# First products of a transform on 64x64 quarters of the array, and maxima spread through free PSUM columns

## The chip, the cores and the metric

One core of a Trainium2 chip runs the kernel alone. The metric is device time in microseconds (us) of one execution; three timed runs of the kernel before gave 3619.89, 3620.4 and 3622.17 us, median 3620.4. The rows below come from one further, profiled execution. PE is TensorE (PEld its weight loads), DVE VectorE, ACT ScalarE, POOL GpSimd, SP the SyncE that issues DMAs.

## The reference

`x` is 8 batches of 3072 x 256. All in float32 accuracy, which the kernel reaches with pairs of fp16 numbers (hi, lo) and three products for each product.

```
X = rfft(x, axis=1)                                  # along the 3072
Yr = Xr @ w_r - Xi @ w_i + b_r ;  Yi = Xr @ w_i + Xi @ w_r + b_i
Y  = soft_threshold(Yr, 0.01) + 1j * soft_threshold(Yi, 0.01)
x  = irfft(Y)                                        # "attn" out, 24576 tokens x 256
x  = (sigmoid(x @ w_gate) * (x @ w_val)) @ w_out     # width 1536
# then 8 experts: tokens with x @ w_skip > 0 go to argmax(x @ w_gate2)
out = x + gate * relu(x @ w1[e]) @ w2[e]             # routed tokens only
```

## The kernel before

The program has three stages. **Boot** transforms batch 0 and prepares the weights. The **main stage** runs 768 *units*: a unit is one of 12 blocks of 128 hidden columns for one of 64 chunks of 384 tokens (8 chunks a batch). `gv` of a unit makes the gate and the value (12 products of 384 columns, tiles `pg`), `out` of the unit two before it makes the output (9 products of 265 columns, tile `pz`); the hidden values go through `h` and `hh` on DVE and ACT. The **last stage** runs the experts in blocks of 512 tokens (`ph`, `py`).

In the main stage a scheduler written in Python, at build time, puts steps of five background tasks behind the products of each unit, up to a budget: `attn` (the transform of the next batch), `y` (its last inverse step, chunk by chunk), `route`, `prep` (expert weights) and `start`. Each task is a generator; a `yield` ends a step, and `k.due` says from which unit on the next may run. Every engine works its instructions in the order in which they were written. When `y` comes to a new batch whose transform is not all written, it names `attn`, and the scheduler writes steps of `attn` at once until it is done.

`attn` of a batch goes through its 8 chunks of `x` (`bound`: the largest magnitude; `scale`; `halve`: hi and lo into `xh`; `cols`: products with the matrix `c1` into a bank of `pa`, then hi and lo into `ah`, and by DMA to `asc` in DRAM). Then it takes 13 groups of frequencies, three stages in a software pipeline: `freq` (tile `al`, product with `f2s`, result `x`), `mix_pair` or `mix` (products with `wri` and `wse`, soft threshold on DVE through `yf`, `yc`, halves `yn`, four DMAs into `yh`), and `inv` of the group before (product of `yh`, halves `zh`, DMA to `zsc`). `y` loads `zt` from `zsc`.

A maximum over partitions is needed before each scaling. `allpow` rounds the per-partition maximum to a power of two on DVE (two instructions on tile `pp`) and its `spread`, written at the end of the task's next step, is one product `pm<-idb,pp` of 128 columns into a bank of `pa` and a DVE maximum over the 128 columns. `pa` has two banks, shared with all products of the tasks.

Before, `c1` for one of the 32 column groups is 96 x 96 and block diagonal: rows are two halves h of 48 time points, columns two halves of 48 results, so half of its entries serve no purpose.

Of the kernel before, what the change touches and what calls it, by code (L numbers as in the profile page):

```python
# [38 lines left out]
def make_consts():  # L39
# [9 lines left out]
    c1 = np.zeros((2, N1, HN, 2, 2, NK))  # L49
# [3 lines left out]
    for h in range(2):  # L53
        t = th[:, h * HN:(h + 1) * HN]
        c1[h, :, :, 0, h, :] = np.cos(t)
        c1[h, :, :, 1, h, :] = -np.sin(t)
        c2[0, h, :, :, h, :] = (w * np.cos(t)).transpose(2, 1, 0)
        c2[1, h, :, :, h, :] = (-w * np.sin(t)).transpose(2, 1, 0)
        c1[h, :, :, :, h, 0] = alt.T[:, None, :]
        c2[:, h, 0, :, h, :] = w / 2 * alt[:, None, :]  # L60
    c1 = np.stack(hl(c1.reshape(96, HN, 96)), 2)
# [24 lines left out]
    at = np.arange(128).reshape(2, 2, HN).transpose(2, 0, 1).reshape(128)  # L86
    f2 = [m.reshape(128, 128)[at] for m in (fx, su, sv)] + [m.reshape(128, 128)[:, at] for m in (fi, si)]
# [78 lines left out]
def allpow(k, out, in_, lo):  # L166

    p = k.pt.tile([128, 1], F32, tag="pp", name="pp", bufs=6)
    pow2(k, p, in_, lo)

    def spread():
        ps = k.pa.tile([128, 512], F32, tag="pa", name="pm")[:, :128]
        w = p.bitcast(BF16)[:, 1:2].broadcast_to([128, 128])
        k.nc.tensor.matmul(ps, w, k.idb, start=True, stop=True)
        k.V.tensor_reduce(out, ps, axis=AX.X, op=ALU.max)

    (k.late if k.boot else k.later).append(spread)
# [26 lines left out]
def split_far(k, hi, lo, src, scale):  # L204

    n = src.free_size()
    tmp = k.sp0.tile([128, n], F32, tag="tmp", name="tmp", bufs=2)
# [6 lines left out]
def task(gen):  # L214
    return [gen, [], []]


def step(k, r):
# [3 lines left out]
    last, k.later = r[2], []  # L222
# [3 lines left out]
    for f in last:  # L226
        f()
    r[1], r[2] = k.late, k.later
    if got == -1 or isinstance(got, str):
        for f in r[1] + r[2] if got == -1 else ():  # L230
            f()
        return got
# [9 lines left out]
def setup_consts(k):  # L242
    nc, cp, d = k.nc, k.cp, k.d
    ld = lambda name, shape, dt: cp.tile(shape, dt, name=name)
    k.c1 = ld("c1", [4 * NK, HN, 2, 96], F16)
# [225 lines left out]
def attn_gen(k, b):  # L471
# [6 lines left out]
    V.memset(mx[:, 0], 0.0)  # L478
    V.memset(px[:, 2], 0.0)
    x32, xh, ah, xs, als, yhs = k.x32, {}, {}, {}, {}, {}  # L480
# [14 lines left out]
    def load(i):  # L495

        e, c = b + i // NC, i % NC
        if e < NB:
            xv = k.d.x[e].rearrange("(n h j) d -> h n j d", h=2, j=HN)
            pool = k.sp0 if e == 0 and c % 4 == 3 else k.xp  # L500
            x32[e, c] = pool.tile([96, NJ, D], F32, tag="x32", name=f"x32_{e}_{c}", bufs=3 if pool is k.xp else 1)
            for h in range(2):
                nc.sync.dma_start(x32[e, c][h * N1:(h + 1) * N1], xv[h, :, c * NJ:(c + 1) * NJ, :])

    def bound(c, h=None):
        if h is None:
            absmax(k, mx[:96, 0, c:c + 1], x32[b, c], axis=AX.XY)
        else:
            absmax(k, (px if h else mx)[:96, h, c:c + 1], x32[b, c][:, 2 * h:2 * h + 2], axis=AX.XY)
        if h == 1:  # L510
            V.tensor_tensor(mx[:96, 0, c:c + 1], mx[:96, 0, c:c + 1], px[:96, 1, c:c + 1], op=ALU.max)
        if h != 0:
            allpow(k, px[:, 0, c:c + 1], mx[:, 0, c:c + 1], 2.0**-40)

    def scale(c):
        inv_pow2(k, px[:, 1, c:c + 1], px[:, 0, c:c + 1], 9)

    def halve(c):
        xh[c] = k.wp.tile([96, 2, NJ, D], F16, tag="xh", name=f"xh_{b}_{c}")
        x, s = x32.pop((b, c)), px[:96, 1, c:c + 1]  # L520
# [5 lines left out]
    def cols(c, t):  # L526
        if t == 0:
            ah[c] = k.wp.tile([4 * NK, NJ, 2, D], F16, tag="ah", name=f"ah_{b}_{c}")
        out = ah[c][:, 2 * t:2 * t + 2]
        ps = bank()[:4 * NK]  # L530
        for jj in range(2):
# [5 lines left out]
        pv = ps.rearrange("p (j e) -> p j e", j=2)  # L537

        def evict():
            (split_far if b == 0 and t else split)(k, out[:, :, 0], out[:, :, 1], pv, 2.0**-7)  # L540
            if t == 1:
                nc.sync.dma_start(asc[:, c * NJ:(c + 1) * NJ], ah[c])

        after(evict)

    def amax(c):
        absmax(k, px[:4 * NK, 2, c:c + 1], ah.pop(c)[:, :, 0], axis=AX.XY)

    f2s = k.wp.tile([128, 3, 2, 128], F16, tag="f2s", name=f"f2s_{b}", bufs=1)
# [10 lines left out]
    def first_cols():  # L560

        pps, pss = {}, {}

        def top(c):
            absmax(k, mx[:96, 0, c:c + 1], x32[b, c], axis=AX.XY)
# [9 lines left out]

        def products(c):
            ah[c] = k.wp.tile([4 * NK, NJ, 2, D], F16, tag="ah", name=f"ah_{b}_{c}")
            x = xh.pop(c)
            pss[c] = [pool.tile([128, 512], F32, tag=tag, name="ps")[:4 * NK] for pool, tag in ((k.pg, "pg"), (k.pa, "pa"))]
            for j in range(NJ):  # L580
                for i, (a, w) in enumerate(PROD):
                    nc.tensor.matmul(
                        pss[c][j // 2][:, j % 2 * D:(j % 2 + 1) * D], k.c1[:, c * NJ + j, a, :], x[:, w, j, :],
                        start=i == 0, stop=i == 2,
                    )

        def evict(c):
# [1043 lines left out]
```

## Time and profile before

| | |
|---|---|
| median of three timed runs | 3620.4 us |
| profiled execution | 3608.6 us, of which the span from first to last instruction is 3606.8 us |
| PE busy | 3396.6 us, 94% of the span |
| DVE / ACT / POOL busy | 66% / 45% / 17% |
| stages (span's clock) | boot to 215 us, main to 2921 us, experts to the end |

Busy PE is matmul time with overlapping tails, so 94% does not say that PE is 94% used; what counts is where PE's idle time stands and what ended it.

### The profile page before, as it was taken

The page shows a single profiled execution, that of the slowest core. Times are in us where ns is not written, and L with a number is a line of the kernel's source. Part 1 is how long each engine was busy: PE and PEld are TensorE (multiplying, and loading weights), DVE is VectorE, ACT ScalarE, POOL GpSimd, SP SyncE. Part 2 cuts the span into 40 slices and gives each one's busy share as a digit, 9 for nine tenths or more (in the row PEclk, how much of TensorE's full clock was granted, in tenths as well). Part 3 has the DMA queues.
Part 4 walks back from the last instruction along what each step waited for, and adds up shares of the span by engine and source line. Part 5 has one row for each costly group of instructions (what it writes and reads, how often), then busy time and mean ns, then how long its engine had stood idle before and what let it go on. Part 6 is the DMA issues. An engine that isn't in the chain of part 4 may idle for free. (4 is left out here: it accounts for less than half of the span.)

```text
span 3606.8 us, 67115 instructions
## 1 busy us (share of the span) xinstructions
PE 3396.6 (94%) x26190; PEld 2428.2 (67%) x26190; DVE 2369.0 (66%) x5577; ACT 1639.4 (45%) x3220; POOL 625.9 (17%) x613
## 2 busy tenths in 40 slices
PE   5589999998999999999999999999999999999997
PEld 4457766676766666666666767676666766667675
DVE  7767677767766766676767676767645455665553
ACT  4545544554454544454444444544434343333332
POOL 2500100120012001200120012001200121333332
PEclk9889999999999999999999999999999999999999
DMA  6333333223332332232323322323211021444442
GB/s 174 113 103 98 96 88 96 87 78 93 99 99 57 104 92 74 78 88 87 94 64 97 96 74 79 99 67 91 70 32 41 28 86 48 154 145 142 162 164 93
DMA packets 220977, 336.06 MB, mean 93 GB/s; under 512 B 37633, under 2 KB 181763, under 8 KB 213392
## 3 DMA queue, kind: packets, MB, share of 16 engines
q1 hardware_dynamic: 204480, 305.43, 28.0%
q0 software_dynamic: 15744, 25.99, 2.4%
q8 instruction: 206, 3.38, 0.4%
q14 instruction: 115, 0.94, 0.1%
q10 hardware_dynamic: 432, 0.33, 0.0%
HBM read 177.99 MB, written 134.09 MB: 87 GB/s over the span
## 5 line engine op out<-in xcount | busy, mean ns | idle before, releaser
L965 PE MATMUL pg<-yT,wgv 128*128 128x384 f16 x9216 | 1634.5, 327 | 5.3 <-ACT yT L149 3.0
L965 PEld LDWEIGHTS <-wgv 128*128 128x128 f16 x9216 | 892.2, 98 | 536.3 <-issue 16.0
L998 PE MATMUL pz<-wo,hh 128*128 128x265 f16 x6912 | 919.0, 277 | 19.0 <-DVE hh L149 16.2
L149 DVE TENSOR_TENSOR hh<-h,hh 128x384 f16<-128x384 f32 x768 | 438.5, 571 | 589.7 <-ACT hh L149 588.1
L998 PEld LDWEIGHTS <-hh 128*128 128x128 f16 x6912 | 675.5, 98 | 213.8 <-DVE hh L149 21.8
L149 ACT ACTIVATE sg<-pg,ys 128x384 f32<-128x384 f32 x768 | 443.7, 578 | 697.5 <-PE pg L965 695.7
L149 DVE SCALAR_TENSOR_TENSOR h<-pg,sg 128x384 f32<-128x384 f32 x768 | 421.8, 549 | 4.7 <-PE pg L965 4.7
L149 ACT CAST hh<-h 128x384 f16<-128x384 f32 x768 | 386.8, 504 | 44.2 <-DVE h L149 43.6
L149 POOL TENSOR_TENSOR x<-sm,x 128x256 f16<-128x256 f32 x77 | 55.0, 714 | 1826.9 <-ACT x L149 836.5
L1095 POOL DMA_INDIRECT lst<-rent,ridx x192 | 198.2, 1032 | 528.4 <-DVE rent L149 277.2
L1320 PE MATMUL ph<-zT,we 128*128 128x512 f16 (+3 forms) x1344 | 268.2, 358 | 4.8 <-DVE h L149 4.1
L1340 PE MATMUL py<-we,h 128*128 128x256 f16 x2400 | 271.1, 273 | 0.9 <-DVE h L149 0.9
L1340 PEld LDWEIGHTS <-h 128*128 128x128 f16 x2400 | 233.5, 98 | 32.6 <-DVE h L149 1.2
L1320 PEld LDWEIGHTS <-we 128*128 128x128 f16 x1344 | 128.1, 98 | 135.8 <-issue 10.7
L149 PEld LDWEIGHTS <-x 128*128 128x128 f16 x1842 | 181.7, 99 | 42.2 <-issue 15.3
L149 ACT ACTIVATE h<-ph 128x512 f16<-128x512 f32 (+3 forms) x224 | 122.2, 548 | 184.3 <-PE ph L1320 182.2
L149 DVE SCALAR_TENSOR_TENSOR h<-ph,h 128x512 f16<-128x512 f32 (+3 forms) x224 | 140.7, 631 | 63.5 <-ACT h L149 61.8
L1346 POOL DMA_INDIRECT out_dram<-og,ix x100 | 99.6, 996 | 250.4 <-DVE gr L149 69.4
L149 DVE SCALAR_TENSOR_TENSOR og<-py,gr,zg 128x256 f32<-128x256 f32 x100 | 48.3, 483 | 143.8 <-PE py L1340 143.4
L149 PE MATMUL ps<-wri,x 128*128 128x256 f16 x918 | 122.1, 280 | 6.5 <-DVE x L149 5.1
L1276 POOL DMA_INDIRECT zg<-zs,ix x100 | 101.9, 1019 | 125.4 <-DVE zh L149 38.8
L149 PE MATMUL ps<-wse,x 128*128 128x256 f16 x924 | 115.1, 275 | 7.6 <-ACT com L149 5.4
(235 smaller groups left out, 3358.5 us busy)
## 6 DMA issues: line engine op xcount, KB each, us to landing
we<-w SPq DMA_DIRECT2D x56, 1024.0 KB, 5.4
x<-in_x_dram SPq DMA_DIRECT2D x128, 192.0 KB, 4.0
asc<-ah SPq DMA_DIRECT2D x64, 384.0 KB, 3.2
al<-asc SPq DMA_DIRECT2D x192, 128.0 KB, 2.6
zsc<-zh SPq DMA_DIRECT2D x192, 128.0 KB, 2.1
zt<-zsc SPq DMA_DIRECT2D x64, 384.0 KB, 4.2
zs<-zo SPq DMA_DIRECT2D x64, 384.0 KB, 2.7
yh<-yn SPq DMA_DIRECT2D x308, 64.0 KB, 2.0
```

The costliest lines, as they stand in the source:

```text
L149: return f(*a, **kw)
L965: nc.tensor.matmul(ps[:, :CT], k.wgv[:, t, g, a, f * 128:(f + 1) * 128], yT[:, t, w, :], start=n == 0, stop=n == 5)
L998: nc.tensor.matmul(zs[(b, c)][t][:, :ZW], hh[:, a, t * 128:(t + 1) * 128], k.wo[:, f, w, :], start=f == 0 and i == 0, stop=f == NF - 1 and ...
L1095: nc.gpsimd.indirect_dma_start(out=k.lst, out_offset=bass.IndirectOffsetOnAxis(ap=idx[:, t:t + 1], axis=0), in_=ent[:, t, :], in_offset=No ...
L1276: nc.gpsimd.indirect_dma_start(out=st.z[:, q, :], out_offset=None, in_=zs, in_offset=bass.IndirectOffsetOnAxis(ap=st.ix[:, 1, q:q + 1], ax ...
L1320: k.nc.tensor.matmul(ps, st.w[0][:, a, t * FE + f * 128:t * FE + (f + 1) * 128], st.zT[:, t, w, :], start=m == 0, stop=m == 5,)
L1340: k.nc.tensor.matmul(ps[:, :D], st.h[f][:, a, q * 128:(q + 1) * 128], st.w[1][:, w, f * D:(f + 1) * D], start=n == 0, stop=n == 23,)
L1346: k.nc.gpsimd.indirect_dma_start(out=k.d.out, out_offset=bass.IndirectOffsetOnAxis(ap=st.ix[:, 0, q:q + 1], axis=0), in_=o[:, q], in_offse ...
```

## The change

It does six things. (1) `c1` is stored as 48 x 64 blocks (48 columns filled) at partitions 0 and 64; a chunk's `cols` is one step of 24 products of 256 columns, four at a time on different quarters of the array (row half h, column half q), into two banks of `pa`, one for each h, in place of two steps of 6 products of 96 x 96. `x32` buffers are fixed, and their unused partitions are zeroed once by POOL. (2) Of the two banks the second is split by ACT, ACT and POOL (`split_far`) in place of ACT and DVE; `asc` is written by four DMAs of a chunk in place of one. (3) Outside of boot a maximum is queued in `k.spreads`, and `gv` of a unit at least two after it puts the product into columns 384 to 511 of its value bank, which the unit leaves free; DVE reads it behind `h`. (4) The task that needs it waits in `settle`, a step in each unit, until that has been written. (5) `LEAD`, by which `y` is due ahead, goes from 7 to 9, and `y_gen` loses two steps. (6) `route` has two more steps, and its two products and the copy of their result share one.

```diff
 def allpow(k, out, in_, lo):
     p = k.pt.tile([128, 1], F32, tag="pp", name="pp", bufs=6)
     pow2(k, p, in_, lo)
-    (k.late if k.boot else k.later).append(spread)
+    if not k.boot:
+        k.spreads.append(Spread(k, p, out))
+        return k.spreads[-1]
+    k.late.append(lambda: spread(k, p, out))
+def settle(k, s):
+    for _ in range(6):
+        if s in k.spreads:
+            k.due = k.unit + 1
+            yield
+    if s in k.spreads:
+        k.spreads.remove(s)
+        spread(k, s.p, s.out)
...
+    def cols(c, banks):
+        ah[c] = k.wp.tile([128, 2, 2, 2, D], F16, tag="ah", name=f"ah_{b}_{c}")
+        x = xh.pop(c)
+        pss[c] = [pool.tile([128, 512], F32, tag=tag, name="ps") for pool, tag in banks]
+        for j in range(2):
             for i, (a, w) in enumerate(PROD):
-                k.T.matmul(
-                    ps[:, jj * D:(jj + 1) * D], k.c1[:, c * NJ + 2 * t + jj, a, :], xh[c][:, w, 2 * t + jj, :],
-                    start=i == 0, stop=i == 2,
-                )
+                for h in range(2):
+                    r = slice(h * 64, h * 64 + N1)
+                    for q in range(2):
+                        k.T.matmul(
+                            pss[c][h][q * 64:(q + 1) * 64, j * D:(j + 1) * D],
+                            k.c1[r, c * NJ + 2 * q + j, a, :], x[r, w, 2 * q + j, :],
+                            start=i == 0, stop=i == 2,
+                        )
+    def evict(c, h):
+        pv = pss[c][h].rearrange("p (j e) -> p j e", j=2)
+        (split_far if h else split)(k, ah[c][:, h, :, 0], ah[c][:, h, :, 1], pv, 2.0**-7)
+        for q in range(2):
+            nc.sync.dma_start(
+                asc[h * 2 * NK:(h + 1) * 2 * NK, c * NJ + 2 * q:c * NJ + 2 * q + 2], ah[c][q * 64:q * 64 + 2 * NK, h]
+            )
...
+        k.xbuf = [(k.xp if i < 3 else k.sp0).tile([128, NJ, D], F32, name=f"x32_{i}") for i in range(4)]
+        for v in k.xbuf:
+            for p in (32, 96):
+                nc.gpsimd.memset(v[p:p + 32], 0.0)
...
             ps = k.pg.tile([128, 512], F32, tag="pg", name="pg")
+            if g == 1:
+                one = take(ps[:, CT:])
...
         V.scalar_tensor_tensor(h32, pss[1][:, :CT], 2.0**-23, sg, op0=ALU.mult, op1=ALU.mult)
+        if one is not None:
+            V.tensor_reduce(one.out, pss[1][:, CT:], axis=AX.X, op=ALU.max)
+    def take(ps):
+        if k.spreads and k.spreads[0].unit < k.unit - 1:
+            one = k.spreads.pop(0)
+            spread_mult(k, one.p, ps)
+            return one
...
-    LEAD = 7
+    LEAD = 9
```

**Maxima on PE.** PE's rows of the main stage where a maximum is spread (`pp` is its weights): before, between a unit's last output product and a task's products, here those of `xh`.

```order
L998 LDWEIGHTS hh
L998 MATMUL pz<-wo,hh 128x265
L174 LDWEIGHTS pp
L174 MATMUL pm<-idb,pp 128x128
L149 LDWEIGHTS c_113
L149 MATMUL ps<-xh_5_10785,c_113 96x256
```

With the change, PE's rows at such a place, inside the products of `gv`, where the value's six begin:

```order
L986 LDWEIGHTS wgv
L986 MATMUL pg<-yT_0_1815,wgv 128x384
L188 LDWEIGHTS pp
L188 MATMUL pg<-idb,pp 128x128
L986 LDWEIGHTS wgv
L986 MATMUL pg<-yT_0_1815,wgv 128x384
```

The spread moved from behind the products of the unit in whose step it was asked for into a unit two or more later; all 142 of the main stage stand so.

**End of a transform on DVE.** DVE's rows at the end of batch 4's transform (`yf`, `yc`, `yn`: threshold and halves of a group; `zh`: halves of an inverse; each `h<-pg` ends a unit's own products and opens its tasks' work). Before, units 334 to 336:

```order
L149 SCALAR_TENSOR_TENSOR yf<-ps,bs_14343,yf 128x512
L149 TENSOR_SCALAR yc<-yf,bs_14343 128x512
L149 TENSOR_TENSOR yf<-yf,yc 128x512
L149 TENSOR_TENSOR hh<-h_18802,hh 128x384
L149 SCALAR_TENSOR_TENSOR h_18857<-pg,sg 128x384
L149 TENSOR_TENSOR pe<-pe 128x1
L149 SCALAR_TENSOR_TENSOR zh<-ps,zh 128x2x256
L149 TENSOR_TENSOR hh<-h_18857,hh 128x384
L149 SCALAR_TENSOR_TENSOR h_18904<-pg,sg 128x384
L149 SCALAR_TENSOR_TENSOR yT_6_18821<-y_18596,ys_6_18721,yT_6_18821 128x2x384
L149 TENSOR_TENSOR yn<-yf,yn 128x2x256
```

With the change, DVE's rows of unit 346, where `y` asks for the batch:

```order
L152 SCALAR_TENSOR_TENSOR h_19801<-pg,sg 128x384
L152 SCALAR_TENSOR_TENSOR yf<-ps,bs_15201,yf 128x512
L152 TENSOR_SCALAR yc<-yf,bs_15201 128x512
L152 TENSOR_TENSOR yf<-yf,yc 128x512
L152 SCALAR_TENSOR_TENSOR zh<-ps,zh 128x2x256
L152 TENSOR_TENSOR yn<-yf,yn 128x2x256
L152 SCALAR_TENSOR_TENSOR yf<-ps,bs_15201,bb_17192 128x256
L152 TENSOR_SCALAR yc<-yf,bs_15201 128x256
L152 TENSOR_TENSOR yf<-yf,yc 128x256
L152 TENSOR_TENSOR yh<-yf,yh 128x256
L152 SCALAR_TENSOR_TENSOR zh<-ps,zh 128x2x256
L152 SCALAR_TENSOR_TENSOR zh<-ps,zh 128x256
```

Before, a group's chain is spread over some five units; with the change the last steps stand in one unit. On PE that unit's row of task products is `wri` x6, `wse` x12, `yh` x3, `wri` x12, `yh` x6, all behind one `out`. Units 443 and 538 (batches 5 and 6) read the same; units 155, 251 and 635 (batches 2, 3, 7) end with `wri` x12, `yh` x6; unit 68 (batch 1) holds three whole groups (11 pieces of products), and unit 69 opens `y` of that batch with `zt` x24.

**Routing in the expert stage on DVE.** DVE's rows at the second piece of the fifth expert block (`h<-ph` is a piece's work). Before:

```order
L149 TENSOR_TENSOR er<-rc,tcs_40014 128x64
L149 SCALAR_TENSOR_TENSOR og<-py,gr,zg 128x256
L149 SCALAR_TENSOR_TENSOR h_40062<-ph,h_40062 128x512
L149 SCALAR_TENSOR_TENSOR h_40096<-ph,h_40096 128x512
L149 TENSOR_REDUCE gr<-zg 128x2
```

With the change:

```order
L152 SCALAR_TENSOR_TENSOR h_40818<-ph,h_40818 128x512
L152 TENSOR_REDUCE rt_21_40821<-R_36315 128x3
L152 TENSOR_TENSOR rdl_21_40822<-R_36315,rt_21_40821 128x24
L152 TENSOR_SCALAR rw_7_21_40824<-rdl_21_40822 128x24
L152 RECIPROCAL rdl_21_40822<-rdl_21_40822 128x24
L152 TENSOR_TENSOR rdl_21_40822<-rw_7_21_40825,rdl_21_40822 128x24
L152 TENSOR_TENSOR rw_7_21_40824<-rw_7_21_40824,rc 128x24
L152 TENSOR_REDUCE rt_21_40821<-rw_7_21_40824 128x3
L152 TENSOR_TENSOR roh_21_40823<-rw_7_21_40824,rt_21_40821 128x24
```

This goes on for 60 DVE rows before the next `h<-ph` (routing of the last chunk and the first of the rest's tables), and PE has the routing's two products (`roa`) behind the block's first six; before, the same work stood between blocks one to four.

## Rows read from the trace of the kernel before

**Rows 1.** The page: span and busy time.

```profile
span 3606.8 us, 67115 instructions
...
PE 3396.6 (94%) x26190; PEld 2428.2 (67%) x26190; DVE 2369.0 (66%) x5577; ACT 1639.4 (45%) x3220; POOL 625.9 (17%) x613
```

**Rows 2.** Stretches: length, busy time of PE, PEld, DVE, ACT, POOL, clock, DMA.

```profile
0.00:215.00 215.00, 119.57 (x800) 91.84 (x801) 156.46 (x314) 108.29 (x189) 73.43 (x67) 0.87 0.49 137
215.00:2921.00 2706.00, 2613.00 (x20421) 1871.58 (x20419) 1831.04 (x4191) 1300.61 (x2577) 333.03 (x328) 1.00 0.28 81
2921.00:3607.00 686.00, 664.04 (x4973) 464.80 (x4970) 381.49 (x1074) 230.47 (x454) 219.49 (x218) 0.99 0.37 129
```

**Rows 3.** PE's waits in the main stage: us in total, times, longest.

```profile
PE pm L174 <- DVE pp L149: 34.5, 23, 3.0
PE pm L174 <- DVE px L149: 14.9, 7, 6.2
PE pz L998 <- DVE hh L149: 14.6, 16, 2.4
...
PE pm L174 <- DVE psc L149: 1.8, 1, 1.8
```

**Rows 4.** Groups by form: busy us, mean ns of one, idle before.

```profile
L149 PE MATMUL ps<-xh,c 96*96 96x256 f16 x672 | 92.2, 272 | 2.0 <-DVE xh L149 1.5 <-ACT y L149 0.5
...
L149 PE MATMUL ps<-c,zt 96*128 96x96 f16 x1536 | 86.5, 207 | 8.1 <-DMA zt<-zsc 8.1
...
L149 DVE SCALAR_TENSOR_TENSOR ah<-ps,ah 96x512 f16<-96x512 f32 x120 | 82.0, 683 | 45.7 <-ACT ah L149 45.1
...
L149 POOL TENSOR_TENSOR ah<-tmp,ah 96x512 f16<-96x512 f32 x8 | 10.7, 1332 | 30.1 <-ACT ah L149 25.3 <-DVE wf L149 4.8
```

**Rows 5.** PE in order of time, 1197 to 1205 us: start, duration, count.

```profile
1197.16 2.11 PE L965 MATMUL pg<-yT,wgv 128*128 128x384 f16 x12
...
1200.14 0.22 PE L174 MATMUL pm<-idb,pp 128*128 128x128 bf16 x1
1200.20 0.82 PE L149 MATMUL ps<-xh,c 96*96 96x256 f16 x6
...
1203.84 0.67 PE L149 MATMUL ps<-c,zt 96*128 96x96 f16 x12
```

**Rows 6.** All engines in order of time, 339 to 349 us: one group's chain.

```profile
339.84 1.36 PE L149 MATMUL ps<-wse,x 128*128 128x256 f16 x11
...
341.32 0.75 DVE L149 SCALAR_TENSOR_TENSOR yf<-ps,bs,yf 128x512 f32<-128x512 f32 x1
342.11 0.55 DVE L149 TENSOR_SCALAR yc<-yf,bs 128x512 f32<-128x512 f32 x1
342.69 0.69 DVE L149 TENSOR_TENSOR yf<-yf,yc 128x512 f32<-128x512 f32 x1
343.41 0.62 ACT L149 CAST yn<-yf 128x512 f16<-128x512 f32 x1 [0.22 <-DVE yf L149]
...
345.30 0.68 DVE L149 TENSOR_TENSOR yn<-yf,yn 128x512 f16<-128x512 f32 x1
...
346.05 2.46 SPq L794 DMA_DIRECT2D yh<-yn  x4
```

**Rows 7.** The page's DMA issues: median us from issue to landing.

```profile
zt<-zsc SPq DMA_DIRECT2D x64, 384.0 KB, 4.2
...
yh<-yn SPq DMA_DIRECT2D x308, 64.0 KB, 2.0
```

**Rows 8.** Stretches around the longest wait, columns as in rows 2.

```profile
824.50:826.70 2.20, 0.00 (x0) 0.00 (x0) 2.10 (x8) 0.00 (x0) 0.82 (x2) 0.50 0.01 1
826.70:831.30 4.60, 4.59 (x17) 2.35 (x18) 1.29 (x4) 2.13 (x3) 1.89 (x2) 0.50 0.02 4
```

**Rows 9.** DVE's groups by form, 2950 to 3130 us: routing and table.

```profile
L149 DVE TENSOR_TENSOR rw<-rw,rc 128x24 f32<-128x24 f32 x10 | 1.8, 179 | 0.2
```

**Rows 10.** POOL's groups by form, 170 to 185 us: a memset.

```profile
L1106 POOL MEMSET pat<- 128x616 f32 x1 | 0.6, 612 | 0.0
```

More of the change, by code (lines that the diff above doesn't have):

```diff
@@ L206, in split_far @@
     n = src.free_size()
-    tmp = k.sp0.tile([128, n], F32, tag="tmp", name="tmp", bufs=2)
+    tmp = (k.sp0 if k.boot else k.gp).tile([128, n], F32, tag="tmp", name="tmp", bufs=2 if k.boot else 1)
     tmp = tmp.rearrange("p (a e) -> p a e", a=src.shape[1])[:src.shape[0]]
@@ L221, in step @@
     todo, k.late = r[1], []
-    last, k.later = r[2], []
     for f in todo:
@@ L225, in step @@
     got = next(r[0], -1)
-    for f in last:
-        f()
-    r[1], r[2] = k.late, k.later
+    r[1] = k.late
     if got == -1 or isinstance(got, str):
-        for f in r[1] + r[2] if got == -1 else ():
+        for f in r[1] if got == -1 else ():
             f()
@@ L574, in spread @@
             inv_pow2(k, px[:, 1, c:c + 1], px[:, 0, c:c + 1], 9)
[L576 to L587, printed above, removed]
-            for t, ps in enumerate(pss.pop(c)):
-                out = ah[c][:, 2 * t:2 * t + 2]
-                pv = ps.rearrange("p (j e) -> p j e", j=2)
-                (split_far if t else split)(k, out[:, :, 0], out[:, :, 1], pv, 2.0**-7)
-            nc.sync.dma_start(asc[:, c * NJ:(c + 1) * NJ], ah[c])
         for c in range(3):
@@ L605, in first_cols @@
                 scales()
-            products(c)
+            cols(c, ((k.pg, "pg"), (k.pa, "pa")))
             if c + 3 < NC:
@@ L629, in attn_gen @@
         yield
-        bound(0, 0)
-        yield
-        bound(0, 1)
-        yield
-        bound(1, 0)
-        yield
-        bound(1, 1)
-        yield
-        scale(0)
+        for c in range(3):
+            bound(c, 0)
+            yield
+            bound(c, 1)
+            yield
+        yield from scale(0)
         halve(0)
@@ L677, in attn_gen @@
     yield
+    if b:
+        yield from settle(k, top)
     inv_pow2(k, col(4), col(3), 1)
@@ L920, in y_gen @@
     absmax(k, col(0), y32, axis=AX.XY)
-    allpow(k, col(2), col(0), 2.0**-20)
+    top = allpow(k, col(2), col(0), 2.0**-20)
     yield
-    yield 1
+    if boot:
+        yield 1
+    else:
+        yield from settle(k, top)
     inv_pow2(k, col(3), col(2), 14)
@@ L1125, in prep_gen @@
             p = k.pe[:, i, e:e + 1]
-            allpow(k, p, s[:, 0:1], 2.0**-40)
+            top = allpow(k, p, s[:, 0:1], 2.0**-40)
             yield
-            yield
+            yield from settle(k, top)
             inv_pow2(k, s[:, 2:3], p, 4 if i == 0 else 14)
@@ L1368, in build @@
     k.V, k.S, k.T, k.G = (Meter(e, r) for e, r in ((nc.vector, 960.0), (nc.scalar, 1200.0), (nc.tensor, 2400.0), (nc.gpsimd, 960.0)))
-    k.yT, k.st, k.zsc, k.R, k.late, k.later = {}, {}, {}, {}, [], []
+    k.yT, k.st, k.zsc, k.R, k.late, k.spreads, k.unit = {}, {}, {}, {}, [], [], 0
     k.x32, k.zt, k.boot = {}, {}, True
@@ L1544, in build @@
             u += 1
+            k.unit = u
         while "start" in run:
```

115 lines of the change are left out of this document (57 added, 58 removed).

## The prediction

> **What bounds the kernel now.** I read the page first: PE is busy for 3396.6 us of a span of 3606.8 us, DVE for 66% of it [rows 1]. That alone does not name the bound, so I cut the span at the ends of its stages. In the main stage PE is busy for 2613.0 of 2706 us, DVE for 1831.0; in boot PE is busy for barely more than half of the time [rows 2]. So work taken from PE, or a wait of PE taken away, counts in the main stage; in boot it does not, as PE is not what ends last there. The view of waits, held to the main stage, names what PE's idle time there is made of: of 93 us idle, 34.5 + 14.9 + 1.8 = 51.2 us are `pm`, the spread of a maximum, waiting for DVE, in 23 + 7 + 1 = 31 waits; the next cause, the output's wait for `hh`, has 14.6 us [rows 3]. So both parts of the change aim at the stage's bound: one at PE's largest cause of idle time, one at products of PE.
>
> **The maxima.** A spread stands behind the products of the unit in which it is asked for, so PE, which works in order, holds the next unit's products until DVE has its two instructions on `pp`. With the change the spread reads a `pp` made two units earlier. A unit takes at least about 3 us on PE: its 12 products started at 1197.16, and what stands behind the nine of its output at 1200.14 [rows 5]. DVE's work behind one unit is thus done by then, and 51.2 us of waits go. To that comes what a wait costs beyond idle time. A lone product of 128 columns shows 0.22 us [rows 5]; in a stream products follow at their columns: six of 256 columns take 0.82 us where one shows 0.272, so (0.82 - 0.272) / 5 = 0.110 us each [rows 4, 5], and 128 columns 0.055. Each wait loses the difference, 0.165 us of tail, as well: 31 x 0.165 = 5.1. Sum **-56 us**. The 142 spreads still cost 0.055 us of stream each, as before. The DVE maximum is the same instruction as before. What hides the spread's new latency is the time until the value is used: the tasks wait in `settle` for two or three units and are due earlier. If that cover is gone, the tasks themselves come late, and that is the fourth part below.
>
> **The 24 products.** Before, 12 products a chunk at 0.110 us make 1.32 us, with 672 = 56 x 12 in this stage [rows 4]: 74 us. After, there are 24 products and 24 weight loads, and no row shows quarters of the array at work. Bounds from rows: if four run in the time of one, 6 x 0.110 = 0.66 us a chunk, -37 us; if each runs alone, 24 x 0.110 = 2.64 us, +74 us. The nearest row for how fast load and product can follow each other is that of `zt`: 12 in 0.67 us, one 0.207 long, so (0.67 - 0.207) / 11 = 0.042 us a pair [rows 4, 5]. I take 24 x 0.042 = 1.01 us: 56 x (1.32 - 1.01) = **-17 us**. The eight chunks of boot gain nothing, since PE is not what boot waits for.
>
> The Trainium skill, "TensorE: Matmul & The Clock Gate", Part 3 on packing small matmuls, says that matmuls on different tiles of the array run concurrently with starts some 4 ns apart; by it a chunk would take about the 0.66 us above and the sum below would be 20 us lower. No run here shows it yet.
>
> **Other edits.** DVE loses 56 subtractions of 0.683 us, ACT gains 56 casts, POOL 56 subtractions of about 1.33 us [rows 4]; DVE and ACT have a third and half of the stage free, POOL seven eighths [rows 2], and `ah` is next read a unit later: nothing. `asc` takes 168 more DMA issues on SP at some 0.6 us [rows 6]; SP issues nothing PE waits for in that time, nothing. In boot POOL zeroes two pieces of 32 x 1024 for a buffer before its `x` may be loaded: at 0.612 us for 616 columns [rows 10] about 1 us each, 2 us for the first chunk: **+2 us**.
>
> **What is late next.** The chunks' steps, the waits in `settle` and `LEAD` shift the tasks, and the order of instructions shows where: at every batch's end `y` asks for the transform before it is written, and the rest of it stands in one unit, with nothing of the main products between its dependent steps. PE is in order, so the chain is open there. Its length is read from one group [rows 6]: `wse` ends at 341.20, `yf`, `yc`, `yf` end at 343.38, ACT ends `yn` at 344.03. DVE's `yn` came at 345.30 behind other work and takes 0.68; four issues on SP take 2.46, the last starting 1.85 after the first; a landing takes 2.0 [rows 7]. As it ran: 349.9 - 341.2 = 8.7 us from products to `yh`. Packed, without DVE's other work but with `com` on POOL (0.5 later) and two `zsc` issues ahead: 0.5 + 2.2 + 0.6 + 0.7 + 1.2 + 1.85 + 2.0, with the hand-overs about 8.3. In units 346, 443 and 538 the products between are `yh` x3 (0.65) and `wri` x12 (1.32): a stall of 6.3 us each, 19 together. In units 155, 251 and 635 only the last group's short chain is open, five pieces of half the columns, about 0.45 each, less 0.65 of products: 2 us each, 6. In unit 68 three groups follow each other: 8.3 against 6.2 us of products for the first, two overlapping chains of 11.2 against 4.9 for the rest, about 9; and unit 69 needs `zt`, which is the last `zh`, its write (about 2) and a load of 4.2 [rows 7] later, with a unit's 3 us of products between: 5 more. Sum **+40 us**, from 28 (each chain at its best, with queued work done meanwhile) to 60 (each as long as it ran before, with DVE's and SP's queues in it).
>
> The same in the expert stage: routing of the last chunk falls behind by two chunks, and 60 DVE rows of about 0.18 us [rows 9], 10.6 us, stand between the first and second piece of a block, with PE's `roa` products behind the first 13. PE waits there for `h`, two ACT steps and 13 rows, some 4 us, runs three pieces of six products (3.9 us) into three banks, and waits again for the other 47 rows: 9 in all, less what these steps cost in their old places: **+8 us**.
>
> More units hold `wri` and `wse` together than before (24 against 17), each with a wait that I put at one ACT step, 0.6 us [rows 6]: 7 x 0.6 = **+4 us**. After the 6.2 us wait the granted clock was 0.50 (1.2 GHz) for 4.6 us in which PE worked [rows 8], so such a stall costs 2.3 us more; five new ones against some drops that go with the spreads' waits: **+3 us**.
>
> **Sum.** -56 - 17 + 2 + 40 + 8 + 4 + 3 = **-16 us**. The profiled execution was 3608.6 us (1.8 beyond its span) and would be 3592.6; the median of the timed runs lies 11.8 us above it, so **3604 us** is forecast, 3592 to 3613 as its own range.
>
> **Rivals.** (a) Quarters at their floor, 0.66 us a chunk: 3604 - 20 = **3584**. For it: loads of `xh`'s products hide fully at 0.110 us now. Against: no row shows pairs closer than 0.042. (b) The array empties at each change of tile size: two changes a chunk, each a tail of 0.272 - 0.110 = 0.162 us [rows 4, 5] on top of the 1.01: 112 x 0.162 = 18, **3622**, no change. The Trainium skill, "TensorEngine Tiling (Array Packing)", Key Properties, states that changing the tiling mode drains TensorE; no trace here has two modes, so it is neither borne out nor refuted. (c) The spreads' waits come back at `hh`: DVE no longer gets the time in which PE stood, and the output waits instead; at half of the 56, **3632**. For it: `hh` is second among PE's waits [rows 3]; against: DVE has a third of the stage free [rows 2]. (d) The other side: the open chains at the ends of transforms. The place is units 68, 346, 443, 538; the price 40 here, and from 63 on it makes the kernel slower by more than 0.2%; at 70, **3634**. (e) Quarters don't overlap: 24 x 0.110 each chunk, +74 in place of -17, **3695**; the first part then doesn't do what it says.
>
> **Chances.** Forecast 0.38, (a) 0.17, (b) 0.13, (c) 0.14, (d) 0.10, (e) 0.08. Three runs lie within 0.06%, so 0.2%, 7 us, is about what can be told from no change. Faster by over 0.2%: forecast and (a), 0.55. Within: (b), 0.13. Slower: (c), (d), (e), 0.32. A range from 3577 ((a) with chains near their best) to 3642 ((d) or (c) and a little more) leaves out (e) and some of each tail.
>
> **What would show it.** Right: `pg<-idb,pp` without waits; main stage shorter; a chunk's 24 products in about 1 us; single PE waits of 6 us for `yh` at four places, and one for `zt`; a wait of PE for `roa` and then `h` in the fifth expert block. Wrong: 24 products in 2.6 us; `hh` waits well over 30 us; no waits for `yn`'s DMA; or a boot longer by more than 10 us.

## The result and the profile after

The changed kernel ran in 3659.9 us (median of four runs, 3657.3 to 3661.0), the kernel before in 3621.3 beside it: a ratio of 1.0105, interval 1.0087 to 1.0122. So it is slower by 1%, where 3604 us and a gain were forecast; the time lies above the range as well.

The page of the kernel after, the same two lines as [rows 1]:

```profile
span 3658.7 us, 69199 instructions
...
PE 3398.8 (93%) x26957; PEld 2384.6 (65%) x26958; DVE 2349.7 (64%) x5505; ACT 1669.3 (46%) x3276; POOL 699.5 (19%) x677
```

Its three stages, cut where [rows 2] cut them (stretch, length, busy time of PE, PEld, DVE, ACT, POOL, clock, DMA):

```profile
0.00:219.70 219.70, 115.77 (x934) 84.03 (x936) 162.80 (x319) 109.65 (x191) 80.07 (x75) 0.89 0.47 133
219.70:2951.50 2731.80, 2611.33 (x21053) 1835.20 (x21051) 1803.05 (x4092) 1329.61 (x2630) 397.21 (x381) 0.98 0.28 81
2951.50:3659.00 707.50, 671.74 (x4975) 465.41 (x4972) 383.82 (x1097) 230.04 (x455) 222.21 (x221) 0.98 0.35 123
```

Boot is 4.7 us longer, the main stage 25.8, the last stage 21.5. The spans differ by 51.9 us, the medians by 38.6 alone: the profiled execution of before was 12 us quicker than its median. A second profile of before, of 3609.7 us, has the same stages within 2 us. Most of what is too much stands in the last stage. Over all kernels of the next section its length goes with the chip that ran them: in kernels with before's routing, or with the shortened one of no_force_route_zt, it is 572 to 573 us on the chip where before's median is 3613 us, and 580 to 587 on three others; in kernels with the changed routing it is 585 on the first and 594 to 595 on two of the others. Both profiles of before have 573. So some 10 of the 21.5 us are not the change's; 4.7 + 25.8 + 11 = 41.5 us are left beside the 38.6 of the medians. In the main stage PE's busy time fell by 1.7 us and its idle time rose from 93 to 120.5. What the idle time is made of, by PE's waits in that stage, beside [rows 3]:

```profile
PE ps L152 <- DMA yh<-yn: 46.3, 12, 7.8
PE ps L152 <- DVE xh L152: 18.3, 12, 3.4
PE pz L1028 <- DVE hh L152: 11.5, 12, 4.2
PE pg L986 <- ACT sg L152: 10.0, 11, 3.7
PE ps L152 <- ACT xh L152: 5.3, 4, 2.7
...
PE ps L152 <- DMA zt<-zsc: 4.5, 1, 4.5
...
PE pg L188 <- DVE pp L152: 0.3, 1, 0.3
```

The 51 us of `pm` waits are gone: the spread, now a product into `pg`, waits 0.3 us. In their place stand waits that before had next to nothing of: for `yh` to come back by DMA (1.9 us before), for `xh` (1.5), for `sg` (1.7). The longest of the first kind, all engines in order of time:

```profile
2289.80 0.82 PE L152 MATMUL ps<-wse,x 128*128 128x256 f16 x6
...
2291.26 0.75 DVE L152 SCALAR_TENSOR_TENSOR yf<-ps,bs,yf 128x512 f32<-128x512 f32 x1 [2.33 <-POOL yf L152]
...
2293.39 0.62 ACT L152 CAST yn<-yf 128x512 f16<-128x512 f32 x1 [3.51 <-DVE yf L152]
...
2295.15 0.76 DVE L152 TENSOR_TENSOR yn<-yf,yn 128x512 f16<-128x512 f32 x1
...
2295.26 1.26 SPq L875 DMA_DIRECT2D zsc<-zh  x2
...
2296.96 3.25 SPq L812 DMA_DIRECT2D yh<-yn  x4
...
2301.71 2.10 PE L152 MATMUL ps<-yh,f 128*128 128x512 f16 x6 [7.80 <-DMA yh<-yn]
```

This is the open chain of the prediction: 11.1 us from the end of `wse` (2290.62) to `yh`, where 8.3 were estimated. `yn` stood 1.1 us on DVE behind other work, and the four issues took 3.25 us behind two for `zsc`, in place of 2.46 [rows 6]. And the stall has a second price. The same place by stretches (columns as above), where [rows 8] had one such place:

```profile
2290.00:2293.90 3.90, 2.73 (x21) 1.71 (x19) 2.03 (x3) 0.51 (x1) 2.22 (x2) 1.00 0.17 38
2293.90:2301.70 7.80, 0.01 (x1) 0.00 (x0) 3.02 (x6) 1.01 (x3) 2.94 (x3) 0.74 0.28 70
2301.70:2304.40 2.70, 2.69 (x9) 1.35 (x10) 0.56 (x1) 1.10 (x3) 0.00 (x0) 0.50 0.01 0
```

While PE stands, the granted clock falls, and for the next 2.7 us of work it is at 0.50 (1.2 GHz). Of the stretches at that level that begin between 225 and 3000 us, the trace's clock records have 6 before, 23.9 us in all, and 19 after, 95.6 us.

The first products themselves did what they should. PE in order of time around one chunk:

```profile
1247.76 1.19 PE L1028 MATMUL pz<-wo,hh 128*128 128x265 f16 x9
1248.88 0.85 PE L152 MATMUL ps<-xh,c 48*64 48x256 f16 x24
1249.66 1.15 PE L986 MATMUL pg<-yT,wgv 128*128 128x384 f16 x6
...
1254.65 1.19 PE L1028 MATMUL pz<-wo,hh 128*128 128x265 f16 x9
1255.68 1.14 PE L986 MATMUL pg<-yT,wgv 128*128 128x384 f16 x6
```

From the start of nine `wo` products the next product follows after 1.03 us where it is a full-size one, after 1.12 us where it is a small one, so 0.09 us go to enter the small tiles. The 24 products hold the queue for 0.78 us (1248.88 to 1249.66). A chunk thus costs 0.87 us where 1.32 stood before: 56 x 0.45 = 25 us saved, more than the 17 forecast. But the waits above for `xh`, 18.3 + 5.3 = 23.6 us, take that back.

To set causes side by side I give each product of PE its delay: its end less that of the product before, less its columns at 2.4 GHz, under the product that waited or, where it ran without a wait at 1.2 GHz, under the low clock. What every product shows, some 2.5 ns, is left out. For the first products the whole time is given, waits for `xh` and the step back to the next product included. Microseconds, 225 to 2950 us, each good to 1 or 2 us; the right columns are kernels of the next section:

| | before | after | no_force | no_force_ route_zt | lead_10 | spreads_only | spreads_only_ lead_10 |
|---|---|---|---|---|---|---|---|
| spreads | 57.1 | 2.7 | 2.7 | 16.7 | 3.0 | 24.1 | 19.4 |
| first products | 75.4 | 76.6 | 73.6 | 68.0 | 63.3 | 83.3 | 80.3 |
| `yh` | 3.0 | 49.6 | 0.4 | 4.9 | 2.7 | 0.4 | 1.1 |
| `zt` | 0 | 8.4 | 22.2 | 2.3 | 1.7 | 0 | 1.0 |
| gates (`yT`, `sg`) | 2.0 | 16.5 | 11.5 | 39.7 | 22.6 | 10.6 | 12.6 |
| output (`hh`, `R`) | 20.7 | 17.8 | 30.4 | 17.8 | 22.7 | 12.1 | 11.8 |
| `wri`, `wse`, `f2s` | 19.6 | 13.8 | 10.7 | 3.4 | 10.5 | 10.3 | 1.9 |
| low clock | 10.6 | 32.1 | 22.2 | 26.9 | 16.7 | 12.5 | 8.6 |

After less before: -54 for the spreads, +1 for the first products, +47 and +8 for the chains, +15 at the gates, -3 at the output, -6, +22 for the clock. That is +29 for a stage that grew by 26.

The last stage shows the chain foretold for the expert blocks. PE and DVE at its first wait, then the second:

```profile
3165.57 0.19 DVE L152 TENSOR_REDUCE rt<-rw 128x3 f32<-128x24 f32 x1
...
3166.57 0.18 DVE L152 TENSOR_TENSOR roa<-roh,rt 128x24 f16<-128x24 f32 x1
...
3166.81 0.19 PE L1100 MATMUL ps<-roa,m 128*128 128x24 f16 x1 [4.11 <-DVE roa L152]
...
3166.88 5.73 PE L1352 MATMUL ph<-zT,we 128*128 128x512 f16 x18
...
3176.74 5.59 PE L1352 MATMUL ph<-zT,we 128*128 128x512 f16 x14 [4.13 <-DVE h L152]
```

4.1 + 4.1 us: PE stands for the router's products behind DVE's routing rows, then for `h` behind the rest of them.

### The profile page after: what moved, and what is told of

It reads as the page before. It is cut to its first block, busy times and chain, and to the rows that moved or that the text cites. A ratio compares the mean times of both kernels' runs of the same rounds, so it can differ in the third digit from the quotient of the medians.

```text
span 3658.7 us, 69199 instructions
## 1 busy us (share of the span) xinstructions
PE 3398.8 (93%) x26957; PEld 2384.6 (65%) x26958; DVE 2349.7 (64%) x5505; ACT 1669.3 (46%) x3276; POOL 699.5 (19%) x677
## 5 line engine op out<-in xcount | busy, mean ns | idle before, releaser
L986 PE MATMUL pg<-yT,wgv 128*128 128x384 f16 x9216 | 1657.6, 329 | 17.6 <-ACT sg L152 10.0
L1028 PE MATMUL pz<-wo,hh 128*128 128x265 f16 x6912 | 920.9, 278 | 14.9 <-DVE hh L152 11.5
L152 DVE TENSOR_TENSOR hh<-h,hh 128x384 f16<-128x384 f32 x768 | 447.0, 582 | 627.5 <-ACT hh L152 615.0
L1352 PE MATMUL ph<-zT,we 128*128 128x512 f16 (+3 forms) x1344 | 273.5, 361 | 11.8 <-DVE h L152 11.0
L152 POOL TENSOR_TENSOR ah<-tmp,ah 128x512 f16<-128x512 f32 x64 | 73.9, 1154 | 866.0 <-ACT ah L152 649.4
L152 PE MATMUL ps<-yh,f 128*128 128x512 f16 (+1 forms) x312 | 87.2, 392 | 73.7 <-DMA yh<-yn 46.3
```

The lines of the kernel that those rows point to most:

```text
L152: return f(*a, **kw)
L986: nc.tensor.matmul(ps[:, :CT], k.wgv[:, t, g, a, f * 128:(f + 1) * 128], yT[:, t, w, :], start=n == 0, stop=n == 5)
L1028: nc.tensor.matmul(zs[(b, c)][t][:, :ZW], hh[:, a, t * 128:(t + 1) * 128], k.wo[:, f, w, :], start=f == 0 and i == 0, stop=f == NF - 1 and ...
L1352: k.nc.tensor.matmul(ps, st.w[0][:, a, t * FE + f * 128:t * FE + (f + 1) * 128], st.zT[:, t, w, :], start=m == 0, stop=m == 5,)
```

## The experiments

Not all kernels ran on the same chip. The median of before beside them was 3621.3 us for after, 3621.8 for no_force to no_late_spread, 3613.0 for in_turn to spreads_only, 3621.9 for whole_in_pairs and 3617.0 for the last two, so kernels are compared by their ratio to it. "Main" is the time from the first to the last gate product, "last" from there to the end of the span.

| kernel | ratio | interval | main | last |
|---|---|---|---|---|
| before | 1 | | 2841.5 | 572.8 |
| after | 1.0105 | 1.0087 to 1.0122 | 2867.3 | 594.2 |
| no_force | 0.9973 | 0.9964 to 0.9983 | 2822.6 | 594.0 |
| old_route | 1.0131 | 1.0114 to 1.0148 | 2888.3 | 584.0 |
| no_quarters | 1.0141 | 1.0124 to 1.0158 | 2885.3 | 595.0 |
| no_late_spread | 1.0248 | 1.0231 to 1.0265 | 2936.1 | 582.7 |
| in_turn (one run) | 1.0178 | | 2893.3 | 585.1 |
| no_force_route_zt | 0.9958 | 0.9945 to 0.9972 | 2829.2 | 573.3 |
| spreads_only | 0.9889 | 0.9874 to 0.9904 | 2802.7 | 572.3 |
| whole_in_pairs | 1.0034 | 1.0022 to 1.0046 | 2851.0 | 586.6 |
| lead_10 | 0.9886 | 0.9869 to 0.9902 | 2795.7 | 580.4 |
| spreads_only_lead_10 | 0.9854 | 0.9838 to 0.9871 | 2785.1 | 583.5 |

**no_force: the end of a transform is forced only from 14 units before the batch's first use.** In `ys`:

```
                         while b not in k.made:
-                            yield "attn"
+                            if k.unit < b * NU - 14:
+                                k.due = k.unit + 1
+                                yield
+                            else:
+                                yield "attn"
```

> The changed kernel, but y does not make the scheduler write the rest of a transform at once: it asks again in each unit, and forces it only from 14 units before the batch's first use. If the open chains at the ends of transforms are what made the kernel slower, PE's waits for yh fall from about 46 us to under 10, the wait for zt in the main stage goes, and so does part of the stretches at the low clock that follow them: about 60 to 65 us less than the changed kernel's 3660, 3595 to 3600. If the loss comes from ACT and DVE being late for the main products (sg, yT, hh) or from the quarters, the time falls by less than 25 us.

Measured 3612.9 us, 47 below the changed kernel and 0.3% below before. Its waits in the main stage:

```profile
PE ps L152 <- DMA zt<-zsc: 19.1, 7, 6.5
PE ps L152 <- DVE xh L152: 16.1, 13, 3.0
PE pz L1028 <- DVE R L152: 13.9, 11, 2.8
PE pz L1028 <- DVE hh L152: 13.0, 9, 3.3
```

No `yh<-yn` is left among them; in the table of causes `yh` fell by 49 us and the low clock by 10, while `zt` rose by 14 and the output by 13. That is why 47 us came in place of the 60 to 65 expected: the reading back of the values, which follows each end, waits next. So the forced ends alone account for more than the 39 us that the change lost. Rival (d) of the prediction had the place right and not the price: the chains cost 55 us, under the 63 from which on it saw a loss.

**old_route: the routing's steps as before.** Three `yield`s of `route` go, and one comes back to its old place:

```
     nc.tensor.matmul(ps[:, W:2 * W], k.m16[:, 1], oa, start=True, stop=True)
+    yield
     tot = tile_("rtot")
...
     V.tensor_tensor(w1, ps[:, :W], tot, op=ALU.subtract)
-    yield
...
     V.tensor_copy(k.base, et(inc)[:, :, T - 1])
-    yield
...
     V.tensor_reduce(sm, te(w1), axis=AX.X, op=ALU.add)
-    yield
```

> The changed kernel with route's steps as before (two fewer). If the routing that fell behind into the fifth expert block cost the last stage its 21 us, that stage comes back to about 573 us and the time falls by 18 to 21 us, to about 3640; the waits for roa and the following ones for h go. If routing there is hidden behind the experts' products, nothing changes (within 5 us).

A miss: 3668.6 us, 9 above the changed kernel. The last stage became 10.2 us shorter (18 to 21 were expected), close to the 8 of the prediction's sum, but the main stage 21 longer. There the output's wait for `hh` doubled:

```profile
PE ps L152 <- DMA yh<-yn: 49.3, 12, 7.8
PE pz L1028 <- DVE hh L152: 24.7, 18, 2.8
```

Where a whole batch is routed at once, the old steps put more of DVE's rows in one burst in front of `hh`. The trace bears this out in part: 15 of the 24.7 us stand where routing made up most of DVE's rows in the 5 us before, 6 of 11.5 in the changed kernel. That accounts for 9 of the 21 us. I had looked at the last stage alone.

**no_quarters: products on the whole array, all else as changed.**

```
-                for h in range(2):
-                    r = slice(h * 64, h * 64 + N1)
-                    for q in range(2):
-                        k.T.matmul(
-                            pss[c][h][q * 64:(q + 1) * 64, j * D:(j + 1) * D],
-                            k.c1[r, c * NJ + 2 * q + j, a, :], x[r, w, 2 * q + j, :], ...
+                    k.T.matmul(
+                        pss[c][t][:, jj * D:(jj + 1) * D], k.c1[:, c * NJ + 2 * t + jj, a, :], x[:96, w, 2 * t + jj, :], ...
```

> The changed kernel with the first products on 96 x 96 blocks of the whole array again (12 a chunk), all else kept. By the rates in the trace of the changed kernel (0.109 us for four quarters, 0.20 us a chunk for going in and out) a chunk's products lose 0.44 us, so 56 chunks take 25 us more: about 3685. If the products on quarters only wait more for xh, as the time inside them (55 us with 23 us of waits) may say, nothing changes (3660, within 8 us).

3672.8 us, 13 above, between the two expectations: with the rest of the change in place quarters are worth 13 us. The products' saving of 25 us is not wholly seen.

**no_late_spread: quarters with spreads as before** (the spread again a step of its own in `pa` behind the unit's products, `LEAD` 7 and the routing as before).

```
-        k.spreads.append(Spread(k, p, out))
-        return k.spreads[-1]
-    k.late.append(lambda: spread(k, p, out))
+    def spread(): ...
+    (k.late if k.boot else k.later).append(spread)
```

> Quarters and the new order of a chunk's steps kept, but maxima spread as before, y and route and LEAD as before. Then no transform ends in one unit. If the quarters are worth 25 us and the new chunk order costs nothing, the time is 3621 - 25 = 3596; if the waits for xh come with the chunk order, 3615; the waits for the spreads, 51 us before, are back in either case. Slower than 3630 would mean that the quarters or the chunk order did the harm.

A miss again, and the largest: 3711.8 us, 90 above before, where 3596 to 3615 was expected. Two of PE's waits in its main stage, and PE around one chunk there:

```profile
PE pm L177 <- DVE pp L152: 46.9, 31, 4.0
...
PE ps L152 <- DVE px L152: 15.6, 29, 1.7
```

```profile
1276.16 0.22 PE L177 MATMUL pm<-idb,pp 128*128 128x128 bf16 x1
1276.31 0.30 PE L152 MATMUL ps<-xh,c 48*64 48x256 f16 x2
1277.71 0.84 PE L152 MATMUL ps<-xh,c 48*64 48x256 f16 x22 [1.11 <-DVE px L152]
```

The quarters need both `pa` banks at once; the spread has just taken one, so after two products PE waits until DVE has read it (15.6 us in 29 waits). The waits of the spreads themselves are back too. So the two parts of the change lean on each other: quarters fit better once the spreads have left `pa`. The 15.6 us are all of the 90 that this shows; the rest stands in other waits and was not taken apart.

**in_turn: the same 24 products, one quarter after the other.**

```
-        for j in range(2):
-            for i, (a, w) in enumerate(PROD):
-                for h in range(2):
-                    r = slice(h * 64, h * 64 + N1)
-                    for q in range(2):
+        for h in range(2):
+            r = slice(h * 64, h * 64 + N1)
+            for q in range(2):
+                for j in range(2):
+                    for i, (a, w) in enumerate(PROD):
```

> The changed kernel with the order of the first products alone changed: the six products of one quarter follow each other, then the next quarter's, so that no two neighbours in the queue lie on different quarters. Theory: the gain of the quarters is the overlap of four, nothing else; a group of four then takes four columns' pitches (4 x 0.107 us) in place of 0.109 us, 24 products of 256 columns a chunk are 2.56 us against 0.65, and the 56 chunks of the main part cost +107 us, less what they hide of the waits for their input (about 23): 3740 to 3770 us. Rival: the array runs small tiles together only because it is in the small-tile mode, whatever the order, or the gain comes from less to load: then the time stays at 3655 to 3665.

3677.3 us, a ratio of 1.0178: some 26 us above the changed kernel by the ratios, not 107. Neither theory holds. One chunk:

```profile
1259.29 1.19 PE L1028 MATMUL pz<-wo,hh 128*128 128x265 f16 x9
1260.41 1.58 PE L152 MATMUL ps<-xh,c 48*64 48x256 f16 x24
1261.92 1.15 PE L986 MATMUL pg<-yT,wgv 128*128 128x384 f16 x6
```

A chunk holds the queue for 1.51 us in place of 0.78; 24 lone products at 0.109 would be 2.6. The records of the single products hint at why: their starts fall into four rows of six with some 109 to 133 ns between neighbours, and each row begins 248 ns after the one before it, when that one has three products still to start (0, 133, 242, 351, 461, 570 ns; then from 248; from 496; from 745). So PE seems to begin on the next quarter while the last one's products still run, two to three quarters together; the records don't name the quarter, so this is read from the spacing alone. The order matters (56 x 0.73 = 41 us), but less than I held; the main stage grew by 26, so some 15 of the 41 were covered by waits that shrank.

**no_force_route_zt: three repairs.** no_force; the load of `zt` due later; and two of `route`'s three `yield`s left out in the last batch:

```
-                        k.due = b * NU - 2 * NF - LEAD
+                        k.due = max(b * NU - 2 * NF - LEAD, k.unit + 4)
...
...
-    yield
+    if T > NT3:
+        yield
...
-    yield
+    if T > NT3:
+        yield
```

> The changed kernel without the forced end of a transform, with two steps fewer in the routing of the last batch alone (its chunks are routed one by one, and these steps stand between the last unit and the expert stage), and with the first products on the values read back not before four units after they were sent. Theory (open transform ends 47 us, routing 20 us of which the last stage has 10 to 18): the run without the forced end measured 3613; the shorter last routing takes 10 to 18 off, the later read-back 5 to 12 of the 22 us that wait there: 3585 to 3600. Rival: the waits move on to the gates and to the values' products, as they did in the run without the forced end: 3605 to 3615.

3597.5 us, ratio 0.9958. The expectation was worked out from a before of 3621.8 us; on that footing it is 0.9958 x 3621.8 = 3606.6 us, in the rival's range. The delay at `zt` fell by 20 us, and the last stage by 21 to 573.3, of which some 10 are the chip's; but the gates now waited 39.7 us, as the rival had it.

**spreads_only: the late spreads without quarters.** To the repairs above, whole-array products in the order of steps of before:

```
-            cols(c, ((k.pa, "pa"),) * 2)
-            evict(c, 0)
-            evict(c, 1)
-            yield
+            half(c, 0)
             if c > 0:
                 amax(c - 1)
             yield
...
+            half(c, 1)
```

> Late spreads alone: the first products on the whole array in the order of chunks of the kernel before, with its input in 96 rows; the spreads as in the changed kernel; the forced end of a transform, the last routing and the read-back as in the other kernel of this call. Theory: the waits at the spreads were 57 us of the kernel before and 3 of the changed one, and nothing of the quarters is needed for it: 3621 - 54 = 3567, plus the routing's 8 in the main part: 3565 to 3585, and quarters are then worth less than nothing beside it. Rival: the quarters' own saving (25 us of products, 13 measured) is missed: 3595 to 3615.

3570.7 us, ratio 0.9889 (3581.6 with a before of 3621.8), inside the theory's range and 42 us below before. The spreads' gain is thus real, and needs no quarters.

**whole_in_pairs: whole-array products, but the order of steps that quarters need.** It is no_force_route_zt with the edit of no_quarters. Beside spreads_only it fills and empties both banks of a chunk in one step, with three bounds ahead in place of two, and splits the second bank on ACT and POOL.

> The kernel no_force_route_zt with its first products on the whole array, both banks of a chunk still filled and emptied in one step, three bounds ahead; beside spreads_only it differs only in that order of a chunk's steps. With quarters it measured 0.9958 of the kernel before, with whole-array products a half chunk at a time 0.9889. Theory: the quarters save what they save under the changed kernel (13 us), and it is the order of steps which they need (both banks at once, then two evictions on the same engines) that loses 40: then this kernel comes out at 0.9985 to 1.001 of before. Rival: the order costs nothing and small tiles themselves cost some 25 us beside the spreads: 0.987 to 0.991.

1.0034, slightly above the theory's bounds, far from the rival's. Against no_force_route_zt (0.9958) quarters save 0.76%, 27 us: all of the products' saving. Against spreads_only (0.9889) the order of steps loses 1.45%, 52 us. How much of that is the order and how much the second bank's split on ACT and POOL was not tried apart. **after_again**, the changed kernel on the same chip, gave 1.0108, as the first time.

> The changed kernel on the same chip as the one above, so that the two can be set side by side without the difference between chips (the kernel before ran in 3621 us on the first and in 3613 on the second). Both theories: 1.009 to 1.012 of before, as the first time.

**lead_10 and spreads_only_lead_10: the values' transform one unit earlier.** Much of what the order of steps loses was in the waits at the gates: 26 of their 34 us of idle time stand between 575 and 950 us of no_force_route_zt. One of them, PE and the values' own steps:

```profile
788.54 0.83 PE L152 MATMUL ps<-f2s,al 128*128 128x128 f16 x12
...
790.13 0.23 PE L188 MATMUL pm<-idb,pp 128*128 128x128 bf16 x1 [0.76 <-DVE pp L152]
...
792.46 0.28 DVE L152 TENSOR_REDUCE ys<-pm 128x1 f32<-128x128 f32 x1
...
793.02 0.93 ACT L152 ACTIVATE yT<-y,ys 128x768 f16<-128x768 f32 x1 [1.00 <-DVE ys L152]
...
794.01 0.48 PE L986 MATMUL pg<-yT,wgv 128*128 128x384 f16 x1 [3.64 <-ACT yT L152]
```

The unit needs `yT` and its maximum isn't spread yet: `settle` gives up and issues a `pm` product of its own, and PE waits for the split. Seven such `pm` stand in that program's main stage, as many in whole_in_pairs, none in spreads_only, and none with

```
-    LEAD = 9
+    LEAD = 10
```

> The kernel no_force_route_zt with the values' transform started one unit earlier (LEAD 10 in place of 9). There seven of the values' splits, at units 60 to 120, came so late that their maximum was spread by a product of its own at the head of the unit that needed them, and the gates waited 40 us for the split values (11 in spreads_only) at a clock that was low for 78 us of that stretch (34). Theory: these seven are what kept quarters behind whole-array products, so without them the quarters' saving shows: 0.9958 less 25 to 35 us, 0.986 to 0.989 of the kernel before. Rival: the pair order of a chunk's steps (two banks, two evictions, three bounds ahead) costs by itself, and the waits move to the next consumer: 0.993 to 0.996.

> spreads_only with the same one unit more of lead, so that the two orders stand side by side with no late split in either. Theory: nothing was late there but one stop of 7.8 us at the first transform's end, so 0.986 to 0.990; beside the kernel above this tells what quarters are worth at the best order of each. Rival: the shift alone moves both kernels by the same 20 to 30 us: 0.981 to 0.984.

3574.9 us (0.9886) and 3566.1 (0.9854). The first reaches the theory's far bound, 0.7% or 26 us below no_force_route_zt, and its rival falls. But the second, a hair below its range and between the two theories, gained 0.35%, 12 us, by the same shift, without a late split to lose. So the seven late splits were worth 14 to 26 us. The second is the best of all: 51 us below before. With neither kernel late, quarters still come out 9 us behind, run against run without overlap (3573.8 to 3579.9 against 3562.7 to 3567.5). The table of causes has them at 63.3 against 80.3 us for the first products, so 17 saved; the gates, the output and `wri`/`wse` lose 30, the clock 8, and the spreads win 16 back. Their waits side by side, lead_10 first:

```profile
PE ps L152 <- DVE xh L152: 13.6, 8, 3.0
PE pg L986 <- ACT yT L152: 13.1, 2, 8.9
PE pz L1028 <- DVE hh L152: 11.3, 4, 4.4
```

```profile
PE pg L185 <- DVE pp L149: 16.3, 14, 3.8
PE pz L1037 <- DVE hh L149: 8.1, 10, 2.0
PE pg L995 <- ACT sg L149: 6.7, 9, 2.4
```

**before_again**: a second profile of before, 3609.7 us of span, with 2842.6 us of main and 573.1 of last stage.

> The kernel before, for a second profile of it: its first one is 12 us below the median of its runs. If the surplus lies in one stage (the expert stage, whose lists depend on nothing that changes), both theories stand as they are; if the stretch of the layers is 10 us longer here, the growth of that stretch by 26 us in the changed kernel's profile is 10 us too large.

The first of the two cases: the main stage stands as read. Both profiles of before have the short last stage, though, and no profile shows before on a chip with the long one. The main stage's growth of 26 us is therefore checked by the medians: their 38.6 us, less 4.7 of boot and 10 to 12 of routing in the last stage, leave 22 to 24.

## Why the prediction was wrong

**The spreads (-56): right.** -54 in the profile, and alone, with the repairs, 42 us below before.

**The first products (-17): near in size, by luck, and wrong in net.** The quarters' own cost is 0.87 us a chunk, between rival (a) and the forecast's 1.01; they saved 25 us. The 1.01 came from 0.042 us a pair of load and product, read from `zt`; but that is the 96 columns themselves (96 at 2.4 GHz are 0.040 us), not the pace of loads. Measured, four quarters go in 0.109 us, 0.027 a pair, and 0.18 for going in and out come on top, which the forecast had left out: two errors that partly cancel. I costed the evictions and the input at nothing, since DVE, ACT and POOL had time free over the stage. But a whole chunk now wants its `xh` at one point, and its two banks are emptied in one step; 24 us of waits for `xh` came, against 1.5 before. They don't come with the quarters: PE's wait for DVE's `xh` is 18.3 us in the changed kernel and 21.5 in no_quarters. In part they come with the order of steps: 13.0 in whole_in_pairs, 7.4 in spreads_only. A free third of an engine over a stage says nothing of whether it is done at the one moment when PE asks. Of rival (b), 0.09 us to enter the small tiles came true and about as much to leave them (the last product starts at 0.85 - 0.27 = 0.58 us, a group is 0.109 us, and the next product starts at 0.78): 56 x 0.18 = 10 us, not its 18. The Trainium skill, "TensorE: Matmul & The Clock Gate", Part 3, has packed matmuls start some 4 ns apart; the trace agrees, four starts within 10 ns. The Trainium skill, "TensorEngine Tiling (Array Packing)", Key Properties, says that a change of mode drains the array; the 0.09 us each way agree with that.

**The chains (+40): right in place, too small.** 47 for `yh` and 8 for `zt`. The middle three, forecast at 19, took 6.9 + 7.0 + 7.8 = 21.7. Here the prediction added wrongly: the seven terms of its packed chain make 9.05 us and not 8.3, and with 9.05 the three would have been 21. The short ones (units 155, 251, 635), forecast at 2 each, took 5.1, 5.6 and 3.5: 14 in place of 6. Unit 155:

```profile
849.62 0.69 DVE L152 TENSOR_TENSOR yn<-yf,yn 128x512 f16<-128x512 f32 x1
...
854.44 2.08 PE L152 MATMUL ps<-yh,f 128*128 128x512 f16 x6 [5.05 <-DMA yh<-yn]
```

PE did not wait for the last group's short chain but for the group before it, whose `yn` came late on DVE and still had to go by DMA; the prediction had taken that as done. The rest stands at unit 68.

**The clock (+3): the term that failed worst.** +22. I counted five new drops at 2.3 us. The clock records show 19 in place of 6, and they stand not at the chains alone but also at waits for `xh` and at the gates. Each of the seven chains' stalls, 3.5 to 7.8 us long, went with a stretch at 1.2 GHz; the 19 stretches are 95.6 us, 5 us each. I had that price in one row [rows 8] and applied it to one kind of stall.

**The gates (not in the sum): +15.** Waits for `sg` and `yT`, behind the denser steps on ACT and DVE.

**`wri`/`wse` (+4):** they fell, by 6.

**Routing (+8): half seen.** Its last stage cost is 10 to 12 (594.0 against 584.0 on one chip, 585.1 against 573.3 on another); in the main stage the same edit saves 21, by old_route.

**The rest of the last stage** goes with the chip, as the result's section has it: some 10 us between chips at equal routing. On the chips with the long stage 2.5 to 6.8 us of PE's waits there are put down to `issue`, on the other none. What in the chip makes the difference stays open.

**Boot (+2)** was +4.7.

So the sum for the main stage was -26 and came out +26, by 18 at the first products, 15 at the chains, 19 at the clock and 15 at the gates, less some 13 at `wri`/`wse` and the output. The step that failed is the one that costed the quarters' denser steps at nothing and charged the low clock to the chains alone. In its place the runs showed 24 us of waits for `xh`, 15 at the gates and 22 of low clock in the changed kernel, and 52 us for that order of steps among the repaired ones. Why the pair order of steps costs as much as it does is shown in part, by the seven late splits (14 to 26 us of the 52); the other causes are named by the table, not taken away one by one.

## What to carry to other kernels

Work saved on the bounding engine is worth only what its inputs let it keep: before counting a faster product, ask when its operands are written and whether they are now all asked for at one moment. A stall on TensorE can cost twice, its length and the low clock behind it: price both. And of a change with several parts, run each alone: here one was worth 1.5%, the other, with the order of steps that it needs, lost 9 us at best, and a schedule that forced a task to its end hid both.

## What was not expected of the hardware

- Small tiles overlap even when queued one quarter after the other: 24 products in 1.51 us, against 0.78 interleaved and an estimated 2.6 (24 x 0.109) one by one.
- Going between full and small tiles cost about 0.09 us each way.
- How much low clock a few stalls bring: 95.6 us at 1.2 GHz over the main stage, 32 us of delay.
- Kernels with equal routing differ by some 10 us in the last stage between chips, while before's median differs by 4 to 9. The cause is open.
